# Retention plus gated feed-forward on one core: the first four chunks' work re-shared between engines, and the input weights loaded in five pieces

## The chip, the core and the metric

The kernel runs on one core of a Trainium2 chip. The time is the device time of one execution in microseconds (us). A trace's span (first to last instruction) is some 1.7 us shorter than the time of the same run. The granted clock is the share of TensorE's full clock that the profile says it was given. Engines: TensorE (PE in the profile; PEld is its weight load), VectorE (DVE), ScalarE (ACT), GpSimd (POOL), and SyncE (SP), which here only issues loads and stores to one DMA queue.

## The reference

```python
scores = 1/sqrt(D) * q @ k.T                   # batch 8, 8 heads, 576 tokens, head size 64
ret = scores * where(i >= j, gamma[h] ** (i - j), 0)
x = (ret @ v) -> [4608 tokens, 512]
h = x @ w_in                                   # 512 x 2048
out = (h * sigmoid(beta * h)) @ w_out          # 2048 x 512
```

## The kernel before

The 576 tokens of each batch are cut into chunks of 128 (the last one has 64). A chunk goes through these steps, in this order:

- `pre`: q is multiplied by a decay and cast to bf16 (`qn`), k is cast (`kn`), v is multiplied and put into a padded tile (`vpad`).
- `a_T`: TensorE transposes qn and kn into PSUM, the memory that it writes its results to (`T`), a copy brings them to SBUF, the engines' working memory (`qkT`).
- `a_sc`: scores `sc`, masked by VectorE into `R`.
- `a_st`: the running state `st`, copied to `sbd`.
- `a_O`: output `O` = state times q, plus R times v; copied to `xT`, the input of the feed-forward.

The feed-forward takes blocks of 512 tokens: 16 up-projections (`up`, PSUM tile `ph`, then Silu) and the down-projections (`down`, PSUM tile `po`). Weights come in fp32 and are cast to bf16. The first four chunks run as a prologue; all later ones are interleaved with up- and down-projections, at places given by numbers. In the timelines below, TensorE's matmuls stand in the order in which they are written.

```python
for b, c in order[:4]:
    load_chunk(b, c)                # q, k, v: 3 loads of 256 KB, in runs of 256 bytes
...
for g in range(WG):                 # 4 pieces of w_in, 1 MB each
    load_w_in(g)
for b, c in order[4:NQ]:            # chunks 4, 5, 6
    load_chunk(b, c)

def pre(i):
    first = i < 4
    (nc.vector if first else nc.gpsimd).tensor_tensor(qn[:cL], t[:cL, 0], gq_b, ALU.mult)
    if first: nc.scalar.copy(kn[:cL], t[:cL, 1])
    else:     nc.gpsimd.tensor_copy(kn[:cL], t[:cL, 1])
    nc.gpsimd.tensor_tensor(vp4[:cL], ...)
...
warm_up(12); betas(); pre(0); a_T(0); nc.gpsimd.memset(vpads[2][:], 0.0); pre(1)
for i in range(4):
    warm_up(2)                      # matmuls on zeros, meant to keep TensorE's clock up
    a_sc(i); a_st(i)
    if i < 3:
        a_T(i + 1)
        if i < 2: pre(i + 2)
    else:
        cast_w_in(0); warm_up(2)
    a_O(i)

fill = [F(up, 0, fo) for fo in range(FO)]          # the 16 up-projections of block 0
merged(fill, [(2, F(cast_w_in, 1)), (5, F(cast_w_in, 2)), (9, F(cast_w_in, 3))],
       [(5.1 + g / 10, F(load_w_out, g)) for g in range(2)],
       [(9.1 + g / 10, F(load_w_out, g)) for g in range(2, WG)],
       [(9.5, F(pre, 4)), (12, F(a_T, 4)), (14, F(a_sc, 4)), (16, F(a_O, 4))],
       [(9.6, F(pre, 5)), (15, F(a_T, 5)), (16.1, F(a_sc, 5))], [(9.7, F(pre, 6))])
for i in range(5):
    load_next(i)                    # chunks 7 to 11, queued behind all of w_out
a_st(5); a_O(5)
...
# then 16 short up-projections and the first down-projections; to the same numbering belong
streams = [[(4, F(cast_w_out, 0)), (10, F(cast_w_out, 1)), ...],
           [(0, F(a_T, 6)), (4, F(a_sc, 6)), (8, F(a_st, 6)), (8, F(a_O, 6))], attn_steps(7, 23), ...]
```

Of the kernel before, what the change touches and what calls it, by code (L numbers as in the profile page):

```python
# [11 lines left out]
F32 = mybir.dt.float32  # L12
BF16 = mybir.dt.bfloat16
# [6 lines left out]
def kernel(  # L20
# [10 lines left out]
    nc = tc.nc  # L31
    B, H, S, D = q.shape
    d_model = H * D
    d_ff = moe_w_in.shape[1]
    N = B * S
    P = 128
    HP = H // 2
    KO = d_model // P
    FO = d_ff // P
# [9 lines left out]
    stage = ctx.enter_context(tc.tile_pool(name="stage", bufs=2))  # L49
    sb = ctx.enter_context(tc.tile_pool(name="sb", bufs=2))  # L50
# [51 lines left out]
    sbds = [consts.tile([P, HP, P], BF16, name=f"sbd{i}") for i in range(NS)]  # L102
    nc.gpsimd.memset(vpads[0][:], 0.0)
    nc.vector.memset(sbds[0][:], 0.0)
    nc.gpsimd.memset(vpads[1][:], 0.0)
    nc.vector.memset(sbds[1][:], 0.0)


# [3 lines left out]
    rbeta_sb = consts.tile([P, FO], F32, name="rbeta_sb")  # L112
    tiny = consts.tile([P, FO], F32, name="tiny")
    WG = 4
    FG = d_ff // WG
    w_in_r = moe_w_in.rearrange("(ko ki) f -> ki ko f", ki=P)
    w_out_r = moe_w_out.rearrange("(fo fi) n -> fi fo n", fi=P)
    wts = {}

    def load_w_in(g):  # L120
        t = stage.tile([P, KO, FG], F32, name="wt", tag="wt", bufs=4)
        nc.sync.dma_start(t[:], w_in_r[:, :, g * FG:(g + 1) * FG])  # L122
        wts[g] = t

    def cast_w_in(g):
        t = wts.pop(g)
        for ko in range(KO):
            e = nc.gpsimd if ko == KO - 1 else nc.vector
            e.tensor_copy(w_in_sb[:, ko, g * FG:(g + 1) * FG], t[:, ko])

    def load_w_out(g):
        t = stage.tile([P, KO, d_model], F32, name="wt", tag="wt", bufs=4)
        nc.sync.dma_start(t[:], w_out_r[:, g * KO:(g + 1) * KO, :])
        wts[WG + g] = t

    def cast_w_out(g):
        t = wts.pop(WG + g)
        for i in range(KO):
            fo = g * KO + i
            e = nc.gpsimd if i == KO - 1 else nc.vector  # L140
            e.tensor_scalar(w_out_sb[:, fo, :], t[:, i], rbeta_sb[:, fo:fo + 1], None, ALU.mult)  # L141

    for g in range(WG):
        load_w_in(g)
    for b, c in order[4:NQ]:
        load_chunk(b, c)
# [1 line left out]
    def warm_up(n):  # L148
        ph = psum.tile([P, MB], F32, name="ph", tag="mm", bufs=3)
        for _ in range(n):  # L150
            nc.tensor.matmul(ph[:], warm[:, :P], warm[:], start=True, stop=True, skip_group_check=True)

    def betas():
        pb = psum.tile([P, FO], F32, name="pb", tag="T", bufs=1)
        nc.tensor.transpose(pb[:], beta_rows[:], ident_f[:FO, :FO])

        nc.vector.tensor_copy(beta_sb[:], pb[:])
        nc.vector.tensor_tensor(tiny[:], beta_sb[:], beta_sb[:], ALU.mult)
        nc.vector.tensor_scalar(tiny[:], tiny[:], 1e-24, 1e-12, ALU.is_lt, ALU.mult)
        nc.vector.tensor_tensor(beta_sb[:], beta_sb[:], tiny[:], ALU.add)  # L160
        nc.vector.reciprocal(rbeta_sb[:], beta_sb[:])
# [6 lines left out]
    def pre(i):  # L168

        b, c = order[i]  # L170
        c0, cL = chunks[c]
        t = qkv_tiles.pop((b, c))
        first = i < 4
        qn = sb.tile([P, H, D], BF16, name="qn", tag="qn", bufs=3)
        kn = sb.tile([P, H, D], BF16, name="kn", tag="kn", bufs=3)
        vp = vpads[i % NV]

        vp4 = vp.rearrange("p (pr two) (x d) -> p pr (two x) d", two=2, x=2)[:, :, 0::3, :]
        gq_b = gq[:cL, c, :].unsqueeze(2).to_broadcast([cL, H, D])
        gv_b = gv[:cL, c, :].unsqueeze(2).to_broadcast([cL, H, D])  # L180
        (nc.vector if first else nc.gpsimd).tensor_tensor(qn[:cL], t[:cL, 0], gq_b, ALU.mult)  # L181
        if first:
            nc.scalar.copy(kn[:cL], t[:cL, 1])
        else:
            nc.gpsimd.tensor_copy(kn[:cL], t[:cL, 1])  # L185
        nc.gpsimd.tensor_tensor(vp4[:cL], t[:cL, 2].rearrange("p (pr two) d -> p pr two d", two=2),  # L186
                                gv_b.rearrange("p (pr two) d -> p pr two d", two=2), ALU.mult)
        live[i] = dict(qn=qn, kn=kn, vp=vp, vp4=vp4)
# [5 lines left out]
    def a_T(i):  # L194
        b, c = order[i]
        c0, cL = chunks[c]
        L = live[i]
        T = psum.tile([P, 2, HP, P], BF16, name="T", tag="T", bufs=1)
        for j, src in enumerate((L["qn"], L["kn"])):
            for p in range(HP):  # L200
                nc.tensor.transpose(T[:, j, p, :cL],  # L201
                                    src[:cL, 2 * p:2 * p + 2, :].rearrange("p h d -> p (h d)"),
                                    ident[:cL, :cL])
        qkT = sb.tile([P, 2, HP, P], BF16, name="qkT", tag="qkT", bufs=3)
        nc.scalar.copy(qkT[:, :, :, :cL], T[:, :, :, :cL])  # L205
        L["qT"], L["kT"] = qkT[:, 0], qkT[:, 1]

    def a_sc(i):
# [15 lines left out]
    def a_O(i):  # L224
        b, c = order[i]
        c0, cL = chunks[c]
        L = live[i]
        R, vp = L["R"], L["vp"]
        O = psum.tile([P, HP, P], F32, name="O", tag="O", bufs=1)
        n = 0  # L230
        if c > 0:
            for p in range(HP):
                nc.tensor.matmul(O[:, p, :cL], sbds[(i - 1) % NS][:, p, :], L["qT"][:, p, :cL],  # L233
                                 start=(n == 0), stop=False, skip_group_check=True)
                n += 1
        for j in range(2):
            for p in range(HP):
                nc.tensor.matmul(O[:, p, :cL], vp[:cL, 2 * p + j, :], R[:cL, j, p, :cL],  # L238
                                 start=(n == 0), stop=(j == 1), skip_group_check=True)
                n += 1  # L240
        n0 = b * S + c0
        nc.vector.tensor_copy(xT[:, :, n0:n0 + cL], O[:, :, :cL])  # L242
        del live[i]

    def a_st(i):
# [50 lines left out]
    def merged(fill, *streams):  # L296

        todo = sorted((x for st in streams for x in st), key=lambda x: x[0])
        for n, f in enumerate(fill):
            while todo and todo[0][0] <= n:  # L300
                todo.pop(0)[1]()
            f()
        for _, step in todo:
            step()

    def F(f, *a):
        return lambda: f(*a)
# [3 lines left out]
        return [(at - 4, F(pre, i)), (at - 3.9, F(load_next, i)), (at, F(a_T, i)), (at + gap, F(a_sc, i)),  # L311
                (at + 2 * gap, F(a_st, i)), (at + 2 * gap, F(a_O, i))]

    warm_up(12)
    betas()
    pre(0)
    a_T(0)
    nc.gpsimd.memset(vpads[2][:], 0.0)
    pre(1)
    for i in range(4):  # L320
        warm_up(2)
        a_sc(i)
        a_st(i)
        if i < 3:
            a_T(i + 1)
            if i < 2:
                pre(i + 2)
        else:
            cast_w_in(0)
            warm_up(2)  # L330
        a_O(i)

    fill = [F(up, 0, fo) for fo in range(FO)]
    merged(fill, [(2, F(cast_w_in, 1)), (5, F(cast_w_in, 2)), (9, F(cast_w_in, 3))],
           [(5.1 + g / 10, F(load_w_out, g)) for g in range(2)],
           [(9.1 + g / 10, F(load_w_out, g)) for g in range(2, WG)],
           [(9.5, F(pre, 4)), (12, F(a_T, 4)), (14, F(a_sc, 4)), (16, F(a_O, 4))],
# [63 lines left out]
```

## Time and profile before

| | |
|---|---|
| time, median of 3 runs | 338.75 us (338.43 to 338.87) |
| span of the trace, mean granted clock | 337.1 us, 0.994 |
| TensorE busy | 325.6 us, 97% of the span |
| first up-projection | 22.28 us |
| transposes of chunk 4 | 32.99 us |
| first down-projection | 48.78 us |
| from there to the end | 288.3 us |

The first lines are from the page of the kernel before: the span, and three rows over 40 equal slices of 8.4 us. PE is TensorE's busy share in tenths, PEclk its granted clock, DMA the busy share of the core's DMA engines.

```profile
span 337.1 us, 6009 instructions
PE   5979899999999999999999999999999999999995
PEclk9799999999999999999999999999999999999999
DMA  9999999999999737906492549036400100011011
```

TensorE is full from the fourth slice or so to the end: only the opening can move. But the DMA row is full as well, and for much longer, over the first thirteen slices (110 us).

The next lines are TensorE's timeline of the kernel before: start in us, us, engine, line, operation, output<-inputs, count; in brackets, the idle time just before and what ended it.

```profile
10.48 0.61 PE L217 MATMUL sc<-qkT 64*128 64x128 bf16 x8 [0.25 <-ACT qkT L205]
18.79 0.40 PE L217 MATMUL sc<-qkT 64*128 64x128 bf16 x8
22.28 10.52 PE L273 MATMUL ph<-xT,w_in_sb 128*128 128x512 bf16 x48 [1.34 <-DVE xT L242]
32.99 0.29 PE L201 MATMUL T<-ident,qn 64*128 64x64 bf16 x4 [0.18 <-POOL qn L181]
33.54 0.29 PE L201 MATMUL T<-ident,kn 64*128 64x64 bf16 x4 [0.27 <-POOL kn L185]
45.90 0.38 PE L238 MATMUL O<-R,vpad 128*128 128x128 bf16 x4 [0.21 <-DVE R L221]
48.78 6.20 PE L285 MATMUL po<-w_out_sb,gT 128*128 128x512 bf16 x28
```

The first two lines are the scores of chunks 0 and 3. There are two places after the prologue where TensorE waits for something that goes back to a load: chunk 4's qn (and kn), and chunk 6's R. VectorE's timeline of the same kernel:

```profile
42.93 1.71 DVE L141 TENSOR_SCALAR w_out_sb<-wt,rbeta_sb 128x512 bf16<-128x512 f32 x3 [1.47 <-DMA wt<-in_moe_w_out_dram]
44.57 1.27 DVE L221 TENSOR_TENSOR R<-sc,causal 128x512 bf16<-128x512 f32 x2
```

VectorE waits for the first w_out tile to land, casts it, and only then masks R of chunk 6, whose scores had been ready since 43.4 us. The chain of waits that ended last (start, us, what): these are its two longest pieces in the opening, and the last one (which the end of the window, 45 us, cuts short):

```profile
16.56 14.94 DMA qkvn<-in_q_dram
35.56 7.35 DMA wt<-in_moe_w_out_dram
44.64 0.60 DVE R L221
```

Up to 42.9 us the chain runs along the DMA queue (SyncE's issuing of loads, then their landings), but for GpSimd's preparation of chunks 4 and 5 from 31.5 to 35.6 us, and touches none of the prologue's compute. (The step from GpSimd to the w_out load is inferred from nearness in time. SyncE issued that load 0.13 us after it was done with the load before it, so nothing else need have held it.)

### The profile page before, as it was taken

Reading aid. Unit: us, or ns where it says so; the run is one execution under the profiler, and the core shown is the slowest. Engines: PE = TensorE matmul, PEld = TensorE weight load, DVE = VectorE, ACT = ScalarE, POOL = GpSimd, SP = SyncE. Lnnn points to the kernel's source line nnn. Section 1 sums busy time; section 2 is a strip of 40 time slices with the busy share of each in tenths; the row PEclk is TensorE's granted clock in tenths of the full one; section 3 lists DMA queues with packets and bytes.
Section 4 is the critical chain, followed back from the end, with each engine's and each line's share of the span. In section 5 each row is a group of like instructions: output and inputs, shape, how many; then the busy total and the mean of one; then the engine's idle time right before and its main releaser. Section 6 shows DMA issues by size and latency. Waiting matters only on the chain.

```text
span 337.1 us, 6009 instructions
## 1 busy us (share of the span) xinstructions
PE 325.6 (97%) x2455; PEld 174.0 (52%) x2455; DVE 114.0 (34%) x202; ACT 163.1 (48%) x272; POOL 115.0 (34%) x132
## 2 busy tenths in 40 slices
PE   5979899999999999999999999999999999999995
PEld 2644574676554555545555555545555555544442
DVE  4664373623321244213332432223224432320011
ACT  2767671385246623752376227712782257404800
POOL 5224767875324433323334432233333330000000
PEclk9799999999999999999999999999999999999999
DMA  9999999999999737906492549036400100011011
GB/s 173 222 387 212 243 377 214 199 212 229 234 222 246 146 111 172 172 0 158 116 228 48 117 118 214 9 87 159 114 2 31 61 36 0 14 55 57 2 61 63
DMA packets 121979, 46.53 MB, mean 138 GB/s; under 512 B 113232, under 2 KB 113248, under 8 KB 121952
## 3 DMA queue, kind: packets, MB, share of 16 engines
q1 hardware_dynamic: 121920, 46.15, 61.3%
q8 instruction: 19, 0.31, 0.4%
q14 instruction: 8, 0.07, 0.1%
q10 hardware_dynamic: 32, 0.01, 0.0%
HBM read 36.71 MB, written 9.44 MB: 137 GB/s over the span
## 4 chain that ended last, share of the span: by engine, by line
PE 84%; DMA 7%; SPq 4%; issue 1%; DVE 1%; ACT 1%; POOL 0%; POOLq 0%
PE po L285 38%; PE ph L273 32%; DMA qkvn<-in_q_dram 4%; PE O L238 4%; PE T L201 4%; SPq L63 4%; PE sc L217 3%; DMA wt<-in_moe_w_out_dram 2%; PE st L255 2%; PE O L233 2%; SPq L122 1%; ACT gT L275 1%; DVE w_out_sb L141 0%; DVE R L221 0%; ACT qkT L205 0%
## 5 line engine op out<-in xcount | busy, mean ns | idle before, releaser
L273 PE MATMUL ph<-xT,w_in_sb 128*128 128x512 bf16 (+2 forms) x640 | 134.2, 358 | 1.7 <-DVE xT L242 1.7
L285 PE MATMUL po<-w_out_sb,gT 128*128 128x512 bf16 x576 | 133.6, 380 | 0.0
L275 ACT ACTIVATE gT<-ph,beta_sb 128x512 bf16<-128x512 f32 (+2 forms) x160 | 102.0, 645 | 41.2 <-PE ph L273 39.9
L273 PEld LDWEIGHTS <-w_in_sb 128*128 128x128 bf16 x640 | 58.4, 98 | 55.5 <-issue 1.6
L285 PEld LDWEIGHTS <-gT 128*128 128x128 bf16 x576 | 53.3, 98 | 57.9
L221 DVE TENSOR_TENSOR R<-sc,causal 128x512 bf16<-128x512 f32 (+1 forms) x80 | 47.2, 631 | 101.1 <-PE sc L217 101.0
L205 ACT COPY qkT<-T 128x1024 bf16<-128x1024 bf16 (+1 forms) x40 | 36.9, 924 | 68.6 <-PE T L201 68.5
L181 POOL TENSOR_TENSOR qn<-qkvn,gq 128x512 bf16<-128x512 f32 (+1 forms) x36 | 37.9, 1052 | 49.9 <-PE T L201 46.4
L186 POOL TENSOR_TENSOR vpad<-qkvn,gv 128x512 bf16<-128x512 f32 (+1 forms) x40 | 41.6, 1041 | 28.2 <-PE O L238 14.9
L291 DVE COPY ot<-po 128x512 f32<-128x512 f32 x36 | 24.8, 691 | 67.5 <-PE po L285 65.1
L185 POOL CAST kn<-qkvn 128x512 bf16<-128x512 f32 (+1 forms) x36 | 21.9, 608 | 69.5 <-issue 65.7
L261 ACT CAST sbd<-st 64x256 bf16<-64x256 f32 x64 | 23.3, 364 | 43.4 <-PE st L255 42.6
L242 DVE CAST xT<-O 128x512 bf16<-128x512 f32 (+1 forms) x40 | 25.5, 637 | 38.0 <-PE O L238 38.0
L238 PE MATMUL O<-R,vpad 128*128 128x128 bf16 (+1 forms) x320 | 23.7, 214 | 1.4 <-DVE R L221 1.2
L238 PEld LDWEIGHTS <-vpad 128*128 128x128 bf16 (+1 forms) x320 | 18.2, 97 | 2.8 <-issue 2.2
L217 PEld LDWEIGHTS <-qkT 64*128 64x128 bf16 (+1 forms) x320 | 8.9, 98 | 17.3 <-ACT qkT L205 7.1
L201 PE MATMUL T<-ident,qn 128*128 128x128 bf16 (+1 forms) x160 | 15.1, 218 | 2.5 <-DVE qn L181 2.4
L201 PEld LDWEIGHTS <-qn 128*128 128x128 bf16 (+1 forms) x160 | 11.1, 99 | 11.9 <-DVE qn L181 2.4
L217 PE MATMUL sc<-qkT 64*128 64x128 bf16 (+1 forms) x320 | 15.5, 217 | 0.6 <-ACT qkT L205 0.4
L201 PE MATMUL T<-ident,kn 128*128 128x128 bf16 (+1 forms) x160 | 14.9, 216 | 0.3 <-POOL kn L185 0.3
L255 PEld LDWEIGHTS <-kn 128*128 128x128 bf16 x128 | 9.5, 99 | 6.6 <-issue 0.2
L255 PE MATMUL st<-vpad,kn 128*128 128x128 bf16 x128 | 12.7, 222 | 0.0
(40 smaller groups left out, 80.0 us busy)
## 6 DMA issues: line engine op xcount, KB each, us to landing
out_dram<-ot SPq DMA_DIRECT2D x36, 256.0 KB, 2.2
qkvn<-in_q_dram SPq DMA_DIRECT2D x32, 256.0 KB, 4.8
qkvn<-in_k_dram SPq DMA_DIRECT2D x32, 256.0 KB, 5.1
qkvn<-in_v_dram SPq DMA_DIRECT2D x32, 256.0 KB, 5.0
wt<-in_moe_w_in_dram SPq DMA_DIRECT2D x4, 1024.0 KB, 10.6
wt<-in_moe_w_out_dram SPq DMA_DIRECT2D x4, 1024.0 KB, 10.2
qkvn<-in_q_dram SPq DMA_DIRECT2D x8, 128.0 KB, 4.0
qkvn<-in_k_dram SPq DMA_DIRECT2D x8, 128.0 KB, 3.6
```

What stands on the lines that cost most here:

```text
L181: (nc.vector if first else nc.gpsimd).tensor_tensor(qn[:cL], t[:cL, 0], gq_b, ALU.mult)
L186: nc.gpsimd.tensor_tensor(vp4[:cL], t[:cL, 2].rearrange("p (pr two) d -> p pr two d", two=2), gv_b.rearrange("p (pr two) d -> p pr two d", ...
L201: nc.tensor.transpose(T[:, j, p, :cL], src[:cL, 2 * p:2 * p + 2, :].rearrange("p h d -> p (h d)"), ident[:cL, :cL])
L205: nc.scalar.copy(qkT[:, :, :, :cL], T[:, :, :, :cL])
L217: nc.tensor.matmul(sc[j][:cL, p, :cL], L["kT"][r, p, :cL], L["qT"][r, p, :cL], start=True, stop=True, skip_group_check=True)
L221: nc.vector.tensor_tensor(R[:cL, j, :, :cL], sc[j][:cL, :, :cL], m_b, ALU.mult)
L238: nc.tensor.matmul(O[:, p, :cL], vp[:cL, 2 * p + j, :], R[:cL, j, p, :cL], start=(n == 0), stop=(j == 1), skip_group_check=True)
L242: nc.vector.tensor_copy(xT[:, :, n0:n0 + cL], O[:, :, :cL])
L255: nc.tensor.matmul(st[:, p, :], L["kn"][:cL, 2 * p:2 * p + 2, :].rearrange("p h d -> p (h d)"), L["vp4"][:cL, p], start=(c == 0 and p == 0 ...
L273: nc.tensor.matmul(ph[:, :tn], w_in_sb[:, ko, fo * P:(fo + 1) * P], xT[:, ko, x0:x0 + tn], start=(ko == 0), stop=(ko == KO - 1))
L275: nc.scalar.activation(gT[:, fo, t0:t0 + tn], ph[:, :tn], ACT.Silu, scale=beta_sb[:, fo:fo + 1])
L285: nc.tensor.matmul(po[:], gT[:, fo, ms * P:(ms + 1) * P], w_out_sb[:, fo, :], start=(fo == 0), stop=(fo == FO - 1))
```

## The change

Its intent is to get the prologue done sooner. In the first four chunks the queries no longer wait for the keys: each half has its own PSUM tile and its own copy (q on ScalarE, k on VectorE). kn goes from ScalarE to VectorE, most of their xT copies from VectorE to ScalarE; beta and a memset leave chunk 0's way; the chunk loop is put in another order, with other warm-up matmuls (27 instead of 22). The first quarter of w_in comes as two loads of 512 KB, so that its cast can start earlier.

```diff
+    pieces = [(0, 256), (256, 256)] + [(f, 512) for f in range(512, d_ff, 512)]
...
-        if first:
-            nc.scalar.copy(kn[:cL], t[:cL, 1])
-        else:
-            nc.gpsimd.tensor_copy(kn[:cL], t[:cL, 1])
+        (nc.vector if first else nc.gpsimd).tensor_copy(kn[:cL], t[:cL, 1])
...
+        T2 = psum.tile([P, 2, HP, P], BF16, name="T2", tag="mm", bufs=3) if i < 4 else T
+        for j, (src, t) in enumerate(((L["qn"], T), (L["kn"], T2))):
             (four transposes)
+            if i < 4:
+                (nc.vector.tensor_copy if j else nc.scalar.copy)(qkT[:, j, :, :cL], t[:, j, :, :cL])
+        if i >= 4:
+            nc.scalar.copy(qkT[:, :, :, :cL], T[:, :, :, :cL])
...
-        nc.vector.tensor_copy(xT[:, :, n0:n0 + cL], O[:, :, :cL])
+        if i == 3:
+            nc.vector.tensor_copy(xT[:, :2, n0:n0 + cL], O[:, :2, :cL])
+            nc.scalar.copy(xT[:, 2:, n0:n0 + cL], O[:, 2:, :cL])
+        else:
+            (nc.scalar.copy if i < 3 else nc.vector.tensor_copy)(xT[:, :, n0:n0 + cL], O[:, :, :cL])
...
-    warm_up(12)
-    betas()
+    warm_up(10)
     pre(0)
-    (the loop shown above)
+    for i in range(4):
+        a_T(i)
+        warm_up(2)
+        a_sc(i)
+        if i < 3:
+            pre(i + 1)
+        a_st(i)
+        warm_up(1 if i else 2)
+        a_O(i)
+        if i == 0:
+            betas()
+        elif i < 3:
+            warm_up(2)
+    cast_w_in(0)
+    cast_w_in(1)
```

From the first up-projection on, both kernels run the same instructions in the same order, apart from the numbering of the pieces.

More of the change, by code (lines that the diff above doesn't have):

```diff
@@ L104 @@
     nc.vector.memset(sbds[0][:], 0.0)
-    nc.gpsimd.memset(vpads[1][:], 0.0)
+    nc.vector.memset(vpads[1][:], 0.0)
+    nc.vector.memset(vpads[2][:], 0.0)
     nc.vector.memset(sbds[1][:], 0.0)
@@ L114 @@
     WG = 4
-    FG = d_ff // WG
+    pieces = [(0, 256), (256, 256)] + [(f, 512) for f in range(512, d_ff, 512)]
+    NP = len(pieces)
     w_in_r = moe_w_in.rearrange("(ko ki) f -> ki ko f", ki=P)
     w_out_r = moe_w_out.rearrange("(fo fi) n -> fi fo n", fi=P)
-    wts = {}
+    wts, whole = {}, [None]
     def load_w_in(g):
-        t = stage.tile([P, KO, FG], F32, name="wt", tag="wt", bufs=4)
-        nc.sync.dma_start(t[:], w_in_r[:, :, g * FG:(g + 1) * FG])
+        f0, fn = pieces[g]
+        if f0 % 512 == 0:
+            t = stage.tile([P, KO, 512], F32, name="wt", tag="wt", bufs=4)
+            whole[0] = t
+        t = whole[0][:, :, f0 % 512:f0 % 512 + fn]
+        nc.sync.dma_start(t, w_in_r[:, :, f0:f0 + fn])
         wts[g] = t
@@ L126, in cast_w_in @@
         t = wts.pop(g)
+        f0, fn = pieces[g]
         for ko in range(KO):
             e = nc.gpsimd if ko == KO - 1 else nc.vector
-            e.tensor_copy(w_in_sb[:, ko, g * FG:(g + 1) * FG], t[:, ko])
+            e.tensor_copy(w_in_sb[:, ko, f0:f0 + fn], t[:, ko])
     def load_w_out(g):
@@ L133, in load_w_out @@
         nc.sync.dma_start(t[:], w_out_r[:, g * KO:(g + 1) * KO, :])
-        wts[WG + g] = t
+        wts[NP + g] = t
     def cast_w_out(g):
-        t = wts.pop(WG + g)
+        t = wts.pop(NP + g)
         for i in range(KO):
@@ L141, in cast_w_out @@
             e.tensor_scalar(w_out_sb[:, fo, :], t[:, i], rbeta_sb[:, fo:fo + 1], None, ALU.mult)
-    for g in range(WG):
+    for g in range(NP):
         load_w_in(g)
@@ L153, in betas @@
     def betas():
-        pb = psum.tile([P, FO], F32, name="pb", tag="T", bufs=1)
+        pb = psum.tile([P, FO], F32, name="pb", tag="mm", bufs=3)
         nc.tensor.transpose(pb[:], beta_rows[:], ident_f[:FO, :FO])
@@ L198, in a_T @@
         T = psum.tile([P, 2, HP, P], BF16, name="T", tag="T", bufs=1)
-        for j, src in enumerate((L["qn"], L["kn"])):
+        T2 = psum.tile([P, 2, HP, P], BF16, name="T2", tag="mm", bufs=3) if i < 4 else T
+        qkT = sb.tile([P, 2, HP, P], BF16, name="qkT", tag="qkT", bufs=3)
+        for j, (src, t) in enumerate(((L["qn"], T), (L["kn"], T2))):
             for p in range(HP):
-                nc.tensor.transpose(T[:, j, p, :cL],
+                nc.tensor.transpose(t[:, j, p, :cL],
                                     src[:cL, 2 * p:2 * p + 2, :].rearrange("p h d -> p (h d)"),
                                     ident[:cL, :cL])
-        qkT = sb.tile([P, 2, HP, P], BF16, name="qkT", tag="qkT", bufs=3)
-        nc.scalar.copy(qkT[:, :, :, :cL], T[:, :, :, :cL])
+            if i < 4:
+                (nc.vector.tensor_copy if j else nc.scalar.copy)(qkT[:, j, :, :cL], t[:, j, :, :cL])
+        if i >= 4:
+            nc.scalar.copy(qkT[:, :, :, :cL], T[:, :, :, :cL])
         L["qT"], L["kT"] = qkT[:, 0], qkT[:, 1]
@@ L312, in attn_steps @@
                 (at + 2 * gap, F(a_st, i)), (at + 2 * gap, F(a_O, i))]
-    warm_up(12)
-    betas()
+    warm_up(10)
     pre(0)
-    a_T(0)
-    nc.gpsimd.memset(vpads[2][:], 0.0)
-    pre(1)
     for i in range(4):
+        a_T(i)
         warm_up(2)
         a_sc(i)
+        if i < 3:
+            pre(i + 1)
         a_st(i)
-        if i < 3:
-            a_T(i + 1)
-            if i < 2:
-                pre(i + 2)
-        else:
-            cast_w_in(0)
+        warm_up(1 if i else 2)
[3 more added lines that the diff above has]
+        elif i < 3:
             warm_up(2)
-        a_O(i)
+    cast_w_in(0)
+    cast_w_in(1)
     fill = [F(up, 0, fo) for fo in range(FO)]
-    merged(fill, [(2, F(cast_w_in, 1)), (5, F(cast_w_in, 2)), (9, F(cast_w_in, 3))],
+    merged(fill, [(2, F(cast_w_in, 2)), (5, F(cast_w_in, 3)), (9, F(cast_w_in, 4))],
            [(5.1 + g / 10, F(load_w_out, g)) for g in range(2)],
```

## The prediction

> **What bounds the kernel now.** From 46 us on, TensorE is busy without a gap (stretches view: 50.0 of 50.0 us again and again) and the change does not touch that part. Only the opening can move. There the timeline has the four prologue chunks' score matmuls at 10.5, 13.5, 16.1 and 18.8 us, the last xT copy at 21.55 and the first up-projection at 22.28 us. But the opening also has a second limit, the one DMA queue. It is never idle from 2 to 46 us (packet records): 217 GB/s in the 256-byte packets of q/k/v, 387 GB/s in the 2 KB packets of the input weights. That agrees with the Trainium skill, "DMA: Bandwidth & Descriptors", Specifications (below 512 B no line rate). Landings: k of chunk 3 at 16.2 us, v at 17.3, the weight quarters at 20.0, 24.3, 27.0 and 30.5, q of chunk 4 at 31.5. From 24 us on, fifteen of the sixteen parts have landed about 2 us before the last one; the late one follows a 16 KB instruction fetch at 20.1 us. Up-projections run 48 matmuls without a hole from 22.28 to 32.8 us, then TensorE waits 0.18 us for qn of chunk 4 (GpSimd, itself waiting for the DMA until 31.6) and 0.27 us for kn. So TensorE reaches chunk 4 just when its data does. The chain of waits that ended last runs over DMA up to 42.9 us and then over the w_out cast and R of chunk 6; it does not pass through the prologue's compute.
>
> **What the change does.** It takes beta (5 DVE operations, 0.9 us) and one GpSimd memset (0.95 us) out of the way of chunk 0, splits the 1.01 us ACT copy of q and k into halves (0.58 us for 512 columns) on ACT and DVE, and moves kn from ACT (0.62) to DVE (about 0.43, as a weight cast), most xT copies from DVE to ACT (0.69). Chunk 0's scores should start near 7 us instead of 10.5. Per chunk, however, DVE now has R 1.29 + qn 0.68 + kn 0.43 + kT 0.6, and the next chunk's scores depend on all of them: about 3.6 us a chunk, close to the 3.6 us in which a chunk's q, k, v land. The head start shrinks; first up-projection near 21.3 us (20.3 to 22.3), at best 2 us early.
>
> **How much counts.** Little. Starting early, up-projections wait for the second weight quarter (24.3 us plus cast) after four, and reach chunk 4's transposes near 32 us, where q still lands at 31.5 and qn is ready only near 32.9. The order of instructions on TensorE makes it wait there about 1 us; everything after is as before. Up to 0.2 us is won. The two half pieces of w_in are 1 KB packets; between 18 ns at 256 B and 85 ns at 2 KB I estimate 46 ns, so 1 MB lands about 0.25 us later, and so does all behind it. The two cancel.
>
> **Prediction.** 338.6 us, 337.6 to 339.4 in 8 of 10. Faster by over 2%: 0.02; within 2%: 0.96; slower by over 2%: 0.02.
>
> **What would show it.** Scores of chunk 0 near 7 us; chunk 3's near 18.5; first up-projection 20.3 to 22.3 us; a new TensorE hole before the fifth up-projection and one of 0.5 to 1.5 us at chunk 4's transposes; these transposes at 33.0 +- 0.4 us; q of chunk 4 landing at 31.5 +- 0.4.
>
> **What would make it wrong.** The late DMA part no longer late (another fetch time): chunk 4 up to 2 us earlier, 336.8 us. Or holes that bring the half clock ("TensorE: Matmul & The Clock Gate", HAM; this trace shows one such window, 8.5 to 11.9 us, after the hole 6.0 to 8.4) into the up-projections: up to 1.7 us more.

## The result, and the profile after

The changed kernel took 338.92 us (338.66 to 339.19, 4 runs), the one before 338.59 us in the 4 runs counted with it. The ratio is 1.001 with a 95% interval of 0.9992 to 1.0027: the same time. Ratios here are the mean time of one kernel's fast runs over the mean of the other's of the same rounds, so not quite the ratio of the medians.

The changed kernel's page and its TensorE timeline:

```profile
span 336.9 us, 5983 instructions
6.76 0.40 PE L227 MATMUL sc<-qkT 64*128 64x128 bf16 x8
18.15 0.40 PE L227 MATMUL sc<-qkT 64*128 64x128 bf16 x8 [0.16 <-DVE qkT L213]
19.97 0.38 PE L269 MATMUL st<-vpad,kn 128*128 128x128 bf16 x4 [1.42 <-POOL vpad L191]
21.96 10.73 PE L287 MATMUL ph<-xT,w_in_sb 128*128 128x512 bf16 x47 [0.72 <-DVE w_in_sb L137]
33.09 0.29 PE L209 MATMUL T<-ident,qn 64*128 64x64 bf16 x4 [0.40 <-POOL qn L189]
33.64 0.29 PE L209 MATMUL T<-ident,kn 64*128 64x64 bf16 x4 [0.27 <-POOL kn L190]
45.94 0.38 PE L248 MATMUL O<-R,vpad 128*128 128x128 bf16 x4 [0.22 <-DVE R L231]
48.82 6.20 PE L299 MATMUL po<-w_out_sb,gT 128*128 128x512 bf16 x27
```

Chunk 0's scores started at 6.76 us instead of 10.48, a head start of 3.7 us. At chunk 3's scores 0.6 us of it was left (18.15 against 18.79), at the first up-projection 0.32 us (21.96 against 22.28), and at chunk 4's transposes nothing: 33.09 against 32.99. From there on TensorE's events are within 0.11 us of the kernel before, up to the first down-projection.

(Counts such as x47 instead of x48 are records missing from a trace. In this trace 40 matmuls lack one, and some of them leave a false hole of 0.16 us or so that is named "issue"; these holes are not read here.)

Three things took the head start. The first and largest is the pace at which the four chunks arrive. Their k lands at 5.34, 8.96, 12.57 and 16.18 us, 3.6 us apart and within 0.02 us of the kernel before. The changed kernel's scores follow at 6.76, 10.82, 14.45 and 18.15 us, 1.4 to 2.0 us after k each time; the kernel before started 5.1 us after k of chunk 0 and had caught up to 2.6 us at chunk 3. With the shortest of these delays (1.42 us) chunk 3's scores could have started at 17.6 us, 1.2 us ahead of the kernel before: by this estimate 2.5 us of the 3.7 went to the landings. The rest is VectorE's: its round from one cast of kn to the next (13.06 to 16.69 us, with short waits for TensorE) takes 3.6 us as well, and kn of chunk 3 was cast 0.5 us after k had landed. No run tested these two apart.

The second is also on the prologue's side: the state matmul of chunk 3 waited 1.42 us for vpad, because v of chunk 3 landed at 18.72 us and not at 17.31 as before. GpSimd's line for it, then VectorE's lines for the third (chunk 6's R):

```profile
18.87 1.04 POOL L191 TENSOR_TENSOR vpad<-qkvn,gv 128x512 bf16<-128x512 f32 x1 [3.92 <-DMA qkvn<-in_v_dram]
42.98 1.71 DVE L149 TENSOR_SCALAR w_out_sb<-wt,rbeta_sb 128x512 bf16<-128x512 f32 x3 [1.42 <-DMA wt<-in_moe_w_out_dram]
44.61 1.28 DVE L231 TENSOR_TENSOR R<-sc,causal 128x512 bf16<-128x512 f32 x2
```

A load is split in 16 parts. Of v of chunk 3, fifteen had landed at 17.30 us; only the last one was late. The packet records show a 16 KB packet of the instruction queue at 16.20 us that took 1.3 us. In the kernel before, that first instruction fetch came at 20.13 us, and there the last part of the second weight quarter was late. In 12 of the 14 traces, the load that landed next after that first packet had started, or the one behind it, is the first whose last part comes 1.0 us or more after the others (1.4 us here); in the other two (four_pieces, three_moves_before) the last part grew late by 0.3 us. That the same one of the 16 engines serves both the packet and the late part is inferred from this order; the trace doesn't name the engine. In the changed kernel the fetch came earlier, and the late part fell into a load that the prologue waits for.

The third is what the prediction rests on: whatever the prologue gains has to pass chunk 4's transposes, and these wait for the DMA queue. In this trace only the last 0.3 us were left to lose there, so that this gate had to be tested by other runs.

### The profile page after: what moved, and what is told of

Same layout as the page of the kernel before. It is cut to its first block, busy times and chain, and to the rows that moved or that the text cites. A ratio compares the mean times of both kernels' runs of the same rounds, so it can differ in the third digit from the quotient of the medians.

```text
span 336.9 us, 5983 instructions
## 1 busy us (share of the span) xinstructions
PE 322.4 (96%) x2420; PEld 173.8 (52%) x2460; DVE 115.6 (34%) x212; ACT 161.3 (48%) x272; POOL 113.0 (34%) x131
## 3 DMA queue, kind: packets, MB, share of 16 engines
q1 hardware_dynamic: 122448, 46.15, 61.6%
## 4 chain that ended last, share of the span: by engine, by line
PE 84%; DMA 6%; SPq 5%; issue 1%; DVE 1%; ACT 1%; POOL 0%; POOLq 0%
PE po L299 37%; PE ph L287 32%; PE O L248 4%; PE T L209 4%; DMA qkvn<-in_q_dram 4%; SPq L63 4%; PE sc L227 3%; DMA wt<-in_moe_w_out_dram 2%; PE st L269 2%; PE O L243 2%; SPq L129 1%; ACT gT L289 1%; DVE w_out_sb L149 0%; DVE R L231 0%; ACT qkT L215 0%
## 5 line engine op out<-in xcount | busy, mean ns | idle before, releaser
L287 PE MATMUL ph<-xT,w_in_sb 128*128 128x512 bf16 (+2 forms) x623 | 132.6, 357 | 2.2 <-DVE w_in_sb L137 0.7
L299 PE MATMUL po<-w_out_sb,gT 128*128 128x512 bf16 x555 | 130.1, 379 | 1.7 <-issue 1.0
L215 ACT COPY qkT<-T 128x1024 bf16<-128x1024 bf16 (+1 forms) x36 | 32.9, 914 | 65.1 <-PE T L209 65.1
L275 ACT CAST sbd<-st 64x256 bf16<-64x256 f32 x64 | 23.3, 364 | 48.5 <-PE st L269 47.7
L190 POOL CAST kn<-qkvn 128x512 bf16<-128x512 f32 (+1 forms) x36 | 21.9, 609 | 70.5 <-issue 68.7
L256 DVE CAST xT<-O 128x512 bf16<-128x512 f32 (+1 forms) x36 | 22.7, 632 | 37.5 <-PE O L248 37.5
```

Source lines behind the costliest of these rows:

```text
L215: nc.scalar.copy(qkT[:, :, :, :cL], T[:, :, :, :cL])
L287: nc.tensor.matmul(ph[:, :tn], w_in_sb[:, ko, fo * P:(fo + 1) * P], xT[:, ko, x0:x0 + tn], start=(ko == 0), stop=(ko == KO - 1))
L299: nc.tensor.matmul(po[:], gT[:, fo, ms * P:(ms + 1) * P], w_out_sb[:, fo, :], start=(fo == 0), stop=(fo == FO - 1))
```

## The experiments

**The theory (A):** the DMA queue's landings set the times at which TensorE can go on: q of chunk 4 near 31.5 us, and (called A2 from the second set on) the first w_out tile near 43 us, with VectorE's order behind it, and chunk 7 near 53 us. Work done earlier on the engines turns into waiting there. Such a place is called a gate below. **Rivals:** B, the late v of chunk 3 ate the gain, and the prologue is on the critical path; C, the opening is hidden behind the queue altogether; B2, latencies between the engines after 33 us eat it.

The table puts the marks of all traces side by side: times in us from the span's start, landings from the semaphore records. It is to be read with the sections below. The changed kernel itself was timed in the first set alone; the later sets have the kernel before in the same rounds, so that the ratios are safe and a difference to the changed kernel's 338.92 us goes across sets.

| run | v chunk 3 lands | first up | q chunk 4 lands | its transposes | w_out 0 lands | R chunk 6 | first down | span |
|---|---|---|---|---|---|---|---|---|
| before | 17.31 | 22.28 | 31.50 | 32.99 | 42.91 | 44.57 | 48.78 | 337.1 |
| after | 18.72 | 21.96 | 31.60 | 33.09 | 42.95 | 44.61 | 48.82 | 336.9 |
| four_pieces | 17.41 | 21.65 | 31.71 | 33.46 | 43.71 | 45.36 | 49.58 | 337.7 |
| fetch_later | 17.32 | 21.06 | 31.91 | 33.36 | 43.81 | 45.47 | 49.68 | 337.7 |
| ups_late | 18.43 | 24.03 | 30.87 | 34.27 | 42.49 | 44.30 | 49.09 | 337.6 |
| chunk4_first | 17.21 | 20.92 | 28.87 | 30.29 | 43.72 | 45.37 | 49.84 | 338.4 |
| cast_after_R6 | 17.30 | 21.07 | 31.43 | 32.91 | 43.03 | 43.37 | 48.17 | 338.0 |
| three_moves | 17.29 | 21.02 | 31.68 | 33.43 | 43.85 | 45.28 | 50.56 | 338.6 |
| three_moves_before | 17.32 | 23.08 | 31.25 | 35.99 | 42.21 | 45.06 | 49.86 | 338.0 |
| three_moves_fetch | 17.35 | 21.05 | 31.42 | 33.32 | 42.68 | 42.45 | 47.24 | 336.2 |
| chunk7_early | 17.06 | 23.26 | 31.58 | 34.59 | 42.93 | 43.75 | 48.55 | 337.4 |
| light_before (wrong) | 17.24 | 22.20 | 25.53 | 32.65 | 35.53 | 42.68 | 47.48 | 335.6 |
| light_after (wrong) | 17.09 | 23.29 | 26.06 | 34.16 | 35.64 | 44.63 | 49.14 | 337.2 |
| light_fetch_later (wrong) | 17.16 | 20.86 | 25.70 | 31.33 | 35.51 | 41.36 | 46.15 | 334.2 |

### fetch_later: give the prologue back what the late load took

```diff
         a_T(i)
-        warm_up(2)
+        if i != 2: warm_up(2)
         a_sc(i)
...
-        warm_up(1 if i else 2)
+        if i == 3: warm_up(1)
         a_O(i)
...
-        elif i < 3: warm_up(2)
+        elif i == 2: warm_up(2)
```

> The changed kernel with 8 of its 27 warm-up matmuls left out (all between chunk 0's state matmuls and chunk 2's scores), so that TensorE reaches the place at which its first 16 KB instruction fetch was made (about the 115th weight load, 16.2 us) later than v of chunk 3 has landed. Theory A (the head start is lost at chunk 4's transposes, whose data the DMA queue delivers near 31.6 us): v of chunk 3 lands at 17.3 us instead of 18.7, the first up-projection starts near 20.9 us instead of 22.0, TensorE then waits about 1.3 us instead of 0.4 for qn of chunk 4, these transposes stay at 33.1 +- 0.3 us, and the time stays within 0.4 us of the changed kernel (338.5 to 339.2 us). Rival B (the late v of chunk 3 is what ate the gain; the prologue is on the critical path): the first up-projection near 20.9 us as well, but the time falls by about 1 us, to 337.9 us. If the granted clock falls to half in the prologue for want of warm-up matmuls, the run tells nothing about either.

Measured: 339.64 us, ratio to the kernel before 1.0014 (0.9991 to 1.0037). The fetch came at 17.7 us, v of chunk 3 was on time, and the first up-projection started at 21.06 us, 0.9 us earlier than in the changed kernel. The TensorE timeline of this run shows where that went:

```profile
25.82 6.98 PE L287 MATMUL ph<-xT,w_in_sb 128*128 128x512 bf16 x31 [0.36 <-DVE w_in_sb L137]
33.36 0.29 PE L209 MATMUL T<-ident,qn 64*128 64x64 bf16 x4 [0.55 <-POOL qn L189]
46.20 0.38 PE L248 MATMUL O<-R,vpad 128*128 128x128 bf16 x4 [0.53 <-DVE R L231]
49.68 2.54 PE L299 MATMUL po<-w_out_sb,gT 128*128 128x512 bf16 x10
```

Before the fifth up-projection TensorE waited for the weights' cast (0.39 us just ahead of the first line, then 0.36), then 0.55 us for chunk 4, and chunk 4's transposes came at 33.36 us, 0.3 us later than in the changed kernel, as did the landing of its q. Rival B is out: the prologue ended 0.9 us earlier, and the time did not fall to the 337.9 us that B asked for. And the first down-projection came 0.86 us *later* (49.68 against 48.82), by just as much as the first w_out tile landed later (43.81 against 42.95). That is the second gate, of which this run's expectation had said nothing. (What moves this landing between 42.2 and 43.9 us from one trace to the next, see the table, is not shown.)

### ups_late: how much slack is there?

```diff
+    warm_up(14)
     cast_w_in(0)
     cast_w_in(1)
```

> The changed kernel with 14 more warm-up matmuls (3.0 us at 216 ns) between the last prologue chunk and the first up-projection: a measure of the slack. Theory A: there are just the 0.4 us that TensorE waits for qn of chunk 4 and the 0.3 us for kn; the first up-projection starts near 25.0 us, chunk 4's transposes near 35.7 us without a wait, and the time rises by 2.2 to 2.7 us, to about 341.4 us. Rival C (TensorE's opening is wholly hidden behind the DMA queue, which delivers until 46 us): less than 1 us more.

Measured: 339.92 us, ratio 1.0025 (1.0000 to 1.0050). The expectation was missed, by two errors. The delay was smaller than planned: the warm-up matmuls filled about 1 us in which TensorE would have waited for the last xT copy and the cast, so the first up-projection moved by 2.07 us (24.03 against 21.96). And of these 2.07 us most were not paid:

```profile
24.03 10.31 PE L287 MATMUL ph<-xT,w_in_sb 128*128 128x512 bf16 x47
34.27 0.29 PE L209 MATMUL T<-ident,qn 64*128 64x64 bf16 x4
45.98 0.61 PE L248 MATMUL O<-R,vpad 128*128 128x128 bf16 x8
49.09 3.18 PE L299 MATMUL po<-w_out_sb,gT 128*128 128x512 bf16 x13
```

At chunk 4's transposes 1.18 us of the delay were left (no wait in front of them now), at the first down-projection 0.27 us: the wait for R of chunk 6 was gone as well. In the time it is 0.9 us more than the kernel before in the same rounds (means), and 1.0 us more than the changed kernel's median, across sets; the spans differ by 0.7 us. So rival C is nearer the truth than theory A was as first put: a 2 us later start costs about 1 us or less, a 1 us earlier start wins nothing. The opening is gated twice, not once.

### chunk4_first: another order of arrival

```diff
-    for g in range(NP): load_w_in(g)
-    for b, c in order[4:NQ]: load_chunk(b, c)
+    for g in range(NP - 1): load_w_in(g)
+    load_chunk(*order[4])
+    load_w_in(NP - 1)
+    for b, c in order[5:NQ]: load_chunk(b, c)
...
-           [(9.5, F(pre, 4)), (12, F(a_T, 4)), (14, F(a_sc, 4)), (16, F(a_O, 4))],
+           [(6, F(pre, 4)), (9, F(a_T, 4)), (11, F(a_sc, 4)), (13, F(a_O, 4))],
```

> The changed kernel with q, k, v of chunk 4 queued ahead of the last input-weight piece, and chunk 4's steps moved up in TensorE's order (transposes before the 10th up-projection instead of the 13th). Theory A (what arrives on the DMA queue sets the time of each step; only an arrival order that keeps TensorE fed can win): q of chunk 4 lands near 28.5 us, the last weight piece near 32.5 us, the waits for qn and kn of chunk 4 (0.67 us) are gone, chunk 5 comes as before; 0.3 to 0.8 us faster than the changed kernel, 338.1 to 338.6 us. Rival B (the prologue alone counts): no difference, 338.9 us, since the prologue is untouched. Slower than 339.3 us if the last weight piece now comes too late for the 13th up-projection.

Measured: 340.04 us, ratio 1.0035 (1.0011 to 1.0060): slower by a third of a per cent, where 0.3 to 0.8 us less had been expected. The expectation named this way to fail: q of chunk 4 landed at 28.87 us and its transposes ran at 30.29, still with waits of 0.29 and 0.27 us; the last weight piece landed at 33.15 us (30.60 in the changed kernel), and TensorE then waited 1.19 us for its cast. On this full queue, bringing one load forward put another one back.

### four_pieces: the weights in four pieces again

```diff
-    pieces = [(0, 256), (256, 256)] + [(f, 512) for f in range(512, d_ff, 512)]
+    pieces = [(f, 512) for f in range(0, d_ff, 512)]
```

> The changed kernel with the input weights in four pieces again, as before the change. Theory A: packets of 1 KB instead of 2 KB cost 0.1 to 0.3 us of the queue, so that q of chunk 4 lands 0.1 to 0.3 us earlier than the 31.6 us of the changed kernel; the first up-projection starts up to 0.5 us later since the whole first quarter has to be cast after the last xT copy (22.2 to 22.5 us); the time within 0.4 us of the changed kernel. If the pieces were what makes the head start possible, 0.5 us or more slower.

Measured: 339.30 us, ratio 1.0004 (0.9981 to 1.0027). q of chunk 4 landed at 31.71 us, not earlier than the 31.60 of the changed kernel. The 1 KB packets do cost something: in the trace of the changed kernel one takes 51 ns (median) against 88 ns for a 2 KB packet of the other weight pieces, and fifteen parts of the first MB land 2.97 us after those of v of chunk 3, where the next MB takes 2.71 us. So the cost is 0.26 us. The first fifteen parts of chunk 4's q land 0.3 us later than before, too (29.48 against 29.14 us), but the last one, which TensorE waits for, comes 2.1 to 2.4 us after them in both kernels. (In four_pieces one part was 0.5 us late from the second load on, before any fetch, so its fifteen parts can't be compared.) In the time the five pieces alone make no difference that these runs show.

### cast_after_R6: open the second gate

In the four traces before, after, four_pieces and fetch_later, the first down-projection starts 5.87 us after the first w_out tile has landed, to the hundredth, for landings from 42.91 to 43.81 us. What links them is one choice in the order: R of chunk 6 stands behind the cast on VectorE.

```diff
-    streams = [[(4, F(cast_w_out, 0)), ...
+    streams = [[(4.5, F(cast_w_out, 0)), ...
```

> The changed kernel with one line moved: the first w_out cast is put on the engines after the scores of chunk 6, so that VectorE masks R of chunk 6 before the cast and not after it. In all six traces so far the first down-projection starts 5.87 us after the first w_out tile has landed (42.9 to 43.8 us), or later where TensorE itself was late. Theory A2 (two gates: first q of chunk 4, then the first w_out tile, behind whose cast R of chunk 6 stands in VectorE's order): R of chunk 6 starts near 43.6 us instead of 44.6, the waits of chunk 6's second output product (0.5 us in all) are gone, the first down-projection starts near 48.3 us whether w_out lands at 42.9 or at 43.8, and the time falls by 0.4 to 1.0 us against the changed kernel's runs with the same landing. Rival (the landing of w_out gates by itself): the first down-projection still 5.9 us after the landing and no gain.

(The expectation says "in all six traces": four of them show 5.87, in the other two TensorE was late itself, with 6.60 and 6.12.) Measured: 339.72 us, ratio 1.0014 (0.9991 to 1.0036), where 0.4 to 1.0 us less had been expected. The gate opened as A2 says: R started at 43.37 us, there was no wait in front of chunk 6's output product, and the first down-projection came at 48.17 us, 5.14 us after the landing. But the time did not fall, and the TensorE timeline shows why:

```profile
45.06 0.61 PE L248 MATMUL O<-R,vpad 128*128 128x128 bf16 x8
48.17 6.20 PE L299 MATMUL po<-w_out_sb,gT 128*128 128x512 bf16 x27
55.66 0.40 PE L209 MATMUL T<-ident,qn 128*128 128x128 bf16 x4 [1.29 <-POOL qn L189]
56.21 0.40 PE L209 MATMUL T<-ident,kn 128*128 128x128 bf16 x4 [0.16 <-POOL kn L190]
```

There is a third gate, chunk 7. Its q stands on the queue behind all of w_out and landed at 54.18 us. The 0.65 us won at the first down-projection were lost again, and some more, since this time chunk 7 came 1.1 us later than in the changed kernel (where its transposes ran at 54.86 us without a wait).

This run's prologue is, instruction for instruction, that of the changed kernel. Yet its first up-projection started at 21.07 us and not at 21.96: the fetch came 0.17 us later (16.37 against 16.20 us) and hit the load after v of chunk 3. It is a second, unplanned copy of fetch_later, with all warm-up matmuls in place, and chunk 4's transposes came at 32.91 us all the same.

### three_moves, three_moves_before, three_moves_fetch: fill the waits by reordering

```diff
-           (12, F(a_T, 4)), (14, F(a_sc, 4)),                    # one up-projection later
+           (13, F(a_T, 4)), (15, F(a_sc, 4)),
...
     a_st(5)
+    a_T(6)                                                       # was (0, F(a_T, 6)) after a_O(5)
     a_O(5)
...
-    streams = [[(4, F(cast_w_out, 0)), ...
+    streams = [[(4.5, F(cast_w_out, 0)), ...
```

three_moves_fetch has the edit of fetch_later besides.

> The changed kernel with three moves in the instruction order and nothing else: the cast behind R of chunk 6 (as in the run before it), chunk 6's transposes between the state and the output products of chunk 5 (to fill TensorE's 0.7 us wait for R of chunk 5), chunk 4's transposes one up-projection later (to fill the 0.4 us wait for qn). Theory A2: the first down-projection near 47.5 us instead of 48.8; 0.8 to 1.4 us faster than the changed kernel, near 337.8 us. If the queue gates elsewhere, less than 0.4 us.

> The same three moves in the kernel before the change, whose first up-projection starts at 22.3 us instead of 22.0. Theory A2: gains as much from the moves as the changed kernel does (0.8 to 1.4 us), and ends within 0.4 us of it. If the changed prologue is worth something once the gates are loosened: 0.5 us or more behind the changed kernel with the moves.

> The three moves in the variant with 8 fewer warm-up matmuls, whose first up-projection started at 21.1 us. Theory A2: the 0.9 us head start goes into the waits before the fourth to sixth up-projection and at chunk 4's transposes, so within 0.4 us of the changed kernel with the three moves. If the prologue counts once the later gate is open: 0.5 us or more faster than that one.

Measured, in this order: 340.26 us (ratio 1.0034, 1.0011 to 1.0058), 339.87 us (1.0016, 0.9993 to 1.0040) and 339.30 us (1.0008, 0.9988 to 1.0028). No gain in any, and three_moves is slower. One comparison came out on the rival's side: three_moves_fetch is 1.1 us faster than three_moves in the means, and its expectation had said that 0.5 us or more would show that the prologue counts once the later gate is open. Some of the 1.1 us may be the half clock shown next, but three_moves' runs at a mean clock of 0.998 to 1.0 (339.42 to 340.29 us) are slower than most of the other's, too. This stays open. The trace of three_moves shows how a filler turned into a hole (TensorE timeline):

```profile
40.19 0.40 PE L209 MATMUL T<-ident,qn 128*128 128x128 bf16 x4 [1.70 <-POOL qn L189]
42.37 2.33 PE L287 MATMUL ph<-xT,w_in_sb 128*128 128x192 bf16 x16 [0.78 <-DVE xT L256]
```

Chunk 6's transposes, put where they were to fill a wait of 0.7 us, waited 1.70 us for q of chunk 6 themselves. And the 16 matmuls after it took 2.33 us instead of 1.58: TensorE's clock had been halved. The stretches view of three_moves (stretch and its length in us; busy us with counts of PE, PEld, DVE, ACT, POOL; granted clock; DMA share; GB/s):

```profile
39.40:42.80 3.40, 1.67 (x22) 1.38 (x23) 0.87 (x2) 1.01 (x1) 2.33 (x3) 1.00 0.85 297
42.80:46.20 3.40, 3.40 (x28) 2.78 (x26) 0.92 (x2) 1.85 (x5) 1.57 (x1) 0.50 0.92 322
```

TensorE was busy for 1.67 of 3.40 us, and the next 3.41 us were granted half the clock. The Trainium skill, "TensorE: Matmul & The Clock Gate", Part 1, describes this: a window of about 3.4 us in which TensorE's activity decides the clock of what follows. This trace agrees (a stretch of 3.413 us at 0.5), and the throttle came although TensorE was idle for half of the window only.

three_moves_fetch had no such window. Its trace has the shortest span of all with a right result (336.2 us; first down-projection at 47.24), but the five timed runs lie between 339.0 and 339.95 us against 338.02 for the profiled one. A single lucky trace is not a faster kernel.

### The light runs: what if the queue carries less?

```diff
-        nc.sync.dma_start(t, w_in_r[:, :, f0:f0 + fn])
+        nc.sync.dma_start(t[:, :2], w_in_r[:, :2, f0:f0 + fn])
...
-            e.tensor_copy(w_in_sb[:, ko, f0:f0 + fn], t[:, ko])
+            e.tensor_copy(w_in_sb[:, ko, f0:f0 + fn], t[:, ko % 2])       # and the same for w_out
```

These kernels give a wrong result: half of each weight tile is loaded and used twice. The work of all engines stays as it was, the queue has 4 MB less to bring.

light_fetch_later has the edit of fetch_later besides.

> WRONG RESULT ON PURPOSE. The kernel before the change, with only two of the four 128-row slices of each weight tile loaded (the casts read the loaded half twice), so that the DMA queue carries 4 MB less and all that comes after the weights lands 5 us and more earlier; the work of the engines is unchanged. Theory A2 (the DMA queue's landings gate TensorE at chunk 4, at the first w_out tile and at chunk 7): no waits for qn and kn of chunk 4 or 7, R of chunk 6 not behind the w_out cast; first up-projection still at 22.3 us since the prologue's compute sets it; 0.7 to 1.3 us faster than the kernel before. If the queue does not gate, the same time as before.

> WRONG RESULT ON PURPOSE. The same cut of the weight loads in the changed kernel. Theory A2: with the gates gone the head start of the prologue stays: the first up-projection at 21.1 or 21.9 us, according to whether the first instruction fetch delays v of chunk 3, and the same difference (0.4 to 1.2 us) against the cut kernel of before at the first down-projection and in the time. Rival B2 (the head start is lost for another reason, such as latencies between the engines after 33 us): first up-projection earlier, but no difference to the cut kernel of before at the first down-projection.

> WRONG RESULT ON PURPOSE. The same cut in the variant with 8 fewer warm-up matmuls, whose v of chunk 3 is on time. Theory A2: first up-projection near 21.0 us, and 1.0 to 1.4 us less than the cut kernel of before at the first down-projection and in the time; while the uncut kernels did not differ by more than 0.4 us. Rival B2: no difference.

| | time (6 runs, us) | ratio to the kernel before |
|---|---|---|
| light_before | 339.45 (337.33 to 340.38) | 1.0018 (0.9991 to 1.0045) |
| light_after | 337.47 (335.97 to 339.11) | 0.9957 (0.9923 to 0.9990) |
| light_fetch_later | 336.14 (335.98 to 336.26, and one slow run left out of the ratio) | 0.9924 (0.9909 to 0.9939) |

In the traces the head start is now kept. The TensorE timelines of light_before, then of light_fetch_later:

```profile
22.20 10.52 PE L273 MATMUL ph<-xT,w_in_sb 128*128 128x512 bf16 x48 [1.29 <-DVE xT L242]
32.65 0.29 PE L201 MATMUL T<-ident,qn 64*128 64x64 bf16 x4
47.48 2.75 PE L285 MATMUL po<-w_out_sb,gT 128*128 128x512 bf16 x12
```
```profile
20.86 10.53 PE L287 MATMUL ph<-xT,w_in_sb 128*128 128x512 bf16 x48 [0.72 <-DVE w_in_sb L137]
31.33 0.29 PE L209 MATMUL T<-ident,qn 64*128 64x64 bf16 x4
46.15 4.04 PE L299 MATMUL po<-w_out_sb,gT 128*128 128x512 bf16 x18
```

A lead of 1.34 us at the first up-projection is 1.32 us at chunk 4's transposes, 1.33 us at the first down-projection and 1.4 us in the span. With the whole queue, the same prologue was 1.22 us ahead of the kernel before at the first up-projection and 0.90 us behind it at the first down-projection. From the first up-projection to the end the two light traces take the same time, 313.4 and 313.3 us; the kernel before takes 314.8 us with the whole queue. Rival B2 is out in these traces: with the landings out of the way, nothing between the engines after 33 us eats a lead.

One expectation failed. light_before was to be 0.7 to 1.3 us faster than the kernel before, and "the same time as before" was to mean that the queue does not gate. Its profiled run was faster (span 335.6 against 337.1), its timed runs together were not. Their mean granted clocks give a hint: one half-clock window of 3.41 us takes 0.5 x 3.41 / 337 = 0.005 off the mean, and four of the six runs have 0.988 to 0.990, the other two (the profiled one among them) 0.995. So most runs probably had two such windows. The kernel before shows the same: of its 33 runs in the three sets of experiments, ten have 0.990 or less and take 339.6 us in the mean, the other 23 take 338.7 us. Where a second window can lie is seen in three_moves_before, whose trace has it at 22.9 to 26.3 us, after a wait of 1.94 us for xT: the matmuls of its first 13 up-projections took 12.98 us, where they took 11.40 us in the trace of chunk7_early. That it lies there in light_before's slower runs too is inferred from the means, not seen. Part of the 2 to 3 us between the timed light kernels may therefore be this clock, and not the head start alone; the traces, which have no such window among the up-projections, show the head start by itself. The clock does not explain all: light_before's other run at 0.995 took 338.96 us, and its four at 0.988 to 0.990 take 339.9 us in the mean, against 339.3 us for the kernel before at the same clock in the same set. Why the cut did nothing for most runs of the kernel before is not shown; that the queue holds up that kernel rests on its trace alone.

light_after is instructive for its scatter: three runs at 336.0 to 336.3 us, three at 338.7 to 339.1. In its profiled run, a late one, the first up-projection started at 23.29 us, not at the 21.1 or 21.9 us expected, though the prologue is that of the changed kernel. Full clock was granted from 6.7 us on and not from 5.5 us, so chunk 0 ran 0.3 us later; two VectorE operations then met GpSimd's multiply of v. VectorE's timeline of light_after, then of the changed kernel:

```profile
10.11 1.02 DVE L167 TENSOR_SCALAR tiny<-tiny 128x16 f32<-128x16 f32 x1
14.21 1.27 DVE L190 CAST kn<-qkvn 128x512 bf16<-128x512 f32 x1
```
```profile
9.82 0.17 DVE L167 TENSOR_SCALAR tiny<-tiny 128x16 f32<-128x16 f32 x1
13.06 0.42 DVE L190 CAST kn<-qkvn 128x512 bf16<-128x512 f32 x1
```

Each of the two took 0.85 us longer. The Trainium skill, "SBUF — State Buffer", "SBUF: two separate sides", says that VectorE's two-port operations and GpSimd hold one port pair exclusively, and that whichever starts second is blocked for the whole of the other. The trace agrees: GpSimd's operations ran from 10.06 to 11.10 us and from 13.67 to 15.19 us, and the two VectorE operations ended at 11.13 and 15.48 us. (That these two are of the two-port kind the trace does not tell.) The trace of chunk7_early, whose first up-projection is as late (23.26 us), has the same two meetings (1.00 and 1.27 us). The second is with kn, which the change moved to VectorE; no run tested what kn on ScalarE would do.

### chunk7_early: one remedy for each gate

(`load_next(0)`, moved up here, is left out of the loop further down.)

```diff
-           [(9.1 + g / 10, F(load_w_out, g)) for g in range(2, WG)],
+           [(9.1, F(load_w_out, 2)), (9.2, F(load_next, 0)), (9.3, F(load_w_out, 3))],
-           ... (12, F(a_T, 4)), (14, F(a_sc, 4)) ...
+           ... (13, F(a_T, 4)), (15, F(a_sc, 4)) ...
-    streams = [[(4, F(cast_w_out, 0)), ...
+    streams = [[(4.5, F(cast_w_out, 0)), ...
```

> A try at a better kernel (right result): the changed kernel with the w_out cast behind R of chunk 6, chunk 4's transposes one up-projection later, and chunk 7 queued ahead of the last w_out tile, one remedy for each of the three gates. Theory A2: q of chunk 7 lands near 50 us instead of 53, no wait at its transposes; the last w_out tile lands near 55.5 us, just in time; first down-projection near 47.8 us; 0.7 to 1.5 us faster than the changed kernel. It fails if the last w_out tile is late, or if a wait for chunk 5 or 6 brings the half clock, as in the run with three moves.

Measured: 339.07 us, ratio 1.0006 (0.9988 to 1.0024), where 0.7 to 1.5 us less than the changed kernel had been expected. The three gates are open in the trace: no wait at chunk 4, none for R of chunk 6, none at chunk 7, whose q landed at 50.12 us. But this trace fell on the late prologue as well (first up-projection at 23.26 us), and the last w_out tile came late by 0.23 us. The timed runs scatter from 338.1 to 339.7 us. No version beats both kernels.

## Why the prediction was right

- **The time**: 338.6 us predicted (337.6 to 339.4), 338.92 measured. Right, and for the reason given: the head start shrinks in the prologue, because VectorE's work on a chunk takes as long as a chunk's landing, and what is left is lost where TensorE waits for what the queue brings. In the changed kernel's own trace most went the first way (3.1 of 3.7 us up to chunk 3's scores) and only 0.3 us was lost at chunk 4; that chunk 4 also stops a larger lead is shown by fetch_later and cast_after_R6.
- **Prologue**: scores of chunk 0 near 7 us (6.76), of chunk 3 near 18.5 (18.15), first up-projection 20.3 to 22.3 us (21.96). Right in the trace of the changed kernel; but the same prologue gave 20.9 to 23.3 us in other traces, so the range was a little narrow, and 21.96 came about by a delay that was not foreseen (v of chunk 3 late after an instruction fetch). Without that delay the same prologue gave 21.07 us in cast_after_R6, nearer to the 21.3 predicted; with the late prologue of chunk7_early the mark would have been missed, so some luck is in it.
- **Chunk 4**: q landing at 31.5 +- 0.4 us (31.60), transposes at 33.0 +- 0.4 (33.09). Right; these two did not follow the prologue in any run with the whole queue and an earlier first up-projection and unchanged place of the transposes (32.91 to 33.46 us for first up-projections from 21.06 to 22.28).
- **The holes**: "a new TensorE hole before the fifth up-projection and one of 0.5 to 1.5 us" at chunk 4. The first was absent and the second only 0.40 us, because the head start was 0.3 us and not 1 us. Both appear where the head start is about 1.2 us (0.39 + 0.36 us and 0.55 us in fetch_later).
- **The 0.25 us for 1 KB packets**: an estimated 46 ns a packet, measured 51 ns, and 0.26 us in the landings of the first MB. But at the landing that counts, that of the last part, little of it was visible (31.60 against 31.50 us; four_pieces 31.71). That "up to 0.2 us won, 0.25 us lost" came out right as a sum is partly luck, since its second term did not matter there.
- **"Everything after is as before"**: right, but there is a further reason beside the one given. The prediction named the chain over the w_out cast and R of chunk 6, and did not use it. It is a second gate, which in four traces put the first down-projection 5.87 us after a landing; behind it stands a third one at chunk 7. A prologue that had got past chunk 4 would have met these.
- **What would make it wrong**: the fetch did move, by 4 us (20.13 to 16.20 us), but it did not make chunk 4 earlier: the last part stayed about 2 us late (31.60 against 29.48 us for the others).

What stays open: whether a kernel with all three gates open and a steady prologue would be faster. chunk7_early's trace had the gates open and an unsteady prologue. Open too are the 1.1 us between three_moves_fetch and three_moves, and why the cut queue did not make most runs of the kernel before faster.

## What to carry to other kernels

Before you speed up a stage, ask of the stages after it which of their inputs is a load, and when it lands: a lead is worth only as much as the next landing lets through, and there may be several such gates one behind the other. Delay the stage on purpose, or cut the queue's bytes in a kernel with a wrong result, and the trace tells you whether there is slack; reordering the full queue only moved the wait here (chunk4_first). For differences below 0.5%, read single events in the traces and several runs, since the same prologue shifted by 2.4 us from trace to trace (20.92 to 23.29 us). The traces point to clock windows, instruction fetches and the port shared by VectorE and GpSimd; no run tested these one by one.

## What the Trainium skill lacked or had wrong

- "Runtime: NRT & Kernel Launch", Instruction fetch mechanics, calls the cost of a 16 KiB instruction block "mostly hidden". Here each of the 14 traces has 19 such packets on the core's instruction queue, and the first four took 0.9 to 1.8 us each. The last of a load's 16 parts was late from the first fetch on: by 1.4 us at v of chunk 3 in the changed kernel, and still by 2.1 us at q of chunk 4. That the fetches cause this is inferred from the order of events, as said above. No page says how large a delay they put on the data loads that a kernel waits for.
- "TensorE: Matmul & The Clock Gate", Part 1, gives the rule of thumb of an idle window (and a case of many short idles, without their share). Here a window in which TensorE was half busy (1.67 of 3.40 us) was followed by a half-clock window too. That the windows run freely is stated; what it may make of a tuned prologue is a first up-projection anywhere from 20.9 to 23.3 us with the same instructions, together with the fetch; in the two late ones (23.26 and 23.29 us) the full clock came 1.1 us later than in the changed kernel's trace (21.96 us).
- "DMA: Bandwidth & Descriptors" states 512 B as the least size for line rate, and the first trace agrees for 256 B (217 GB/s against 387 GB/s). It gives no time of a packet for the sizes just above it on this chip; here a packet of 1 KB took 51 ns and one of 2 KB 88 ns, 16% more per byte, and the 1 MB in 1 KB packets landed 0.26 us later than a MB in 2 KB packets (2.97 against 2.71 us).
